# Groups of 768 tokens in an attention and feed-forward kernel: a fourth accumulator, other places for attention work and output stores

## The chip, the cores and the metric

The kernel runs on one core of a Trainium2 chip. The metric is the device time of one execution in microseconds (us): three timed executions of the kernel before took 904.45, 904.82 and 906.39 us, so the median is 904.82. One execution was also taken with a profile.

## The reference

The first part is a windowed attention over 8 batches, 8 heads, 576 positions and head size 64; the second part sends its output, as 4608 tokens of 512 values, through two matrix products with an ELU between them.

```python
scores = scale * np.matmul(q, k.transpose(0, 1, 3, 2))
scores = np.where(masks[None, :, :, :], scores, -1000000000.0)   # window 32, or 128 with stride 4
attn = np.exp(scores - np.max(scores, axis=-1, keepdims=True))
attn = attn / (np.sum(attn, axis=-1, keepdims=True) + 1e-09)
x = np.matmul(attn, v).transpose(0, 2, 1, 3).reshape(4608, 512)
h = x @ w_in                                                      # 512 x 2048
g = np.where(h > 0.0, h, np.exp(np.minimum(h, 0.0)) - 1.0)
return g @ w_out                                                  # 2048 x 512
```

## The kernel before, in words

The 4608 tokens are worked in three chunks of 512 and then in four large groups of 768, each of them two halves of 384 tokens; the program calls the large ones superchunks, and they are numbered c = 0 to 3 here. Nearly all of the time the matrix engine (TensorE, PE in the profile) multiplies, in a fixed order that the program writes down; VectorE (DVE) and ScalarE (ACT) prepare operands, apply the ELU and do the softmax, and SyncE's queue (SP) issues every DMA. Instructions of PE, and those that go through `vec` and `act`, keep the program's order on their engine. Stores, loads and a few others are placed by the scheduler.

A superchunk has 8 steps q. In each step the first product is formed from seven block products, s = 0 to 6, in the order A11, S2, S3, A12, S1, A22, S4 (`ORDER`). Each is six matmuls of 128x384 on a weight block that is streamed from DRAM (`r<-combined`) through a ring of five slots. A11, S2, S3 and A22 add up in one PSUM tile (`x_ps`, h0). A12, S1 and S4 all use the other tile (`y_ps`, h1): A12 and S1 each start it anew and S4 adds to S1. The four results are made by ACT copies u1, u2, u3 of `x_ps` after s = 0, 1, 2; DVE sums C11 = A12 tile + u1 and C22 = S1 tile + u3; an ACT copy C21 of `x_ps` after s = 5; and the DVE sum C12 = S4's tile + u2. The ELU of one step follows in pieces that `TODO` sets beside the products of this step and the next: exponentials and relus (ACT), `elu` (DVE), `cast` (ACT) and `rest` (DVE), which splits a value in a rounded part and a remainder for the next product.

Between the block products PE takes items of the second product from a queue (`pop(n)`: n items of three matmuls of 128x512). `POPS` says how many after each s. Only half of a step's ELU output is used at once. The other half is stored to DRAM (`keep`, `aside`) and comes back in a loop over 16 blocks f at the end of the superchunk (`bring`), in which PE does only second-product items.

Attention for the later batches is woven in. `PIECES` places a scores piece (S, two head pairs: 24 small matmuls, two pops, 48 more) and an output piece (O, 24 small matmuls on `pt`) by 7q + s. After S, DVE adds masks, subtracts the row maximum; ACT takes the exponential; DVE sums, normalises and transposes; ACT copies six blocks to the tile `pt`, which O reads. `work` hands these steps out after each block product, within the time in `SPARE`; `next_step` lets a DVE step run after an ACT step of the same head pair only one place later. Score results use the PSUM tiles a_ps0, a_ps1 and a third one. Between the two halves of S an ACT copy of one column to the tile `nothing` (L523) reads a score.

A finished output tile (128x512) is copied by ACT from PSUM (L645) into one of a few tiles that are used in turn (`out_tiles`), and SP stores it (L646).

Before the first superchunk the last chunk's blocks f = 12 to 15 share DVE and ACT with the making of the seven moving operands (B11, T2, ...; `SOON`, `NEXT`, `FIRST`) and with the first S piece (`EARLY`). `flush` sets how many blocks' second products are left waiting; 16 items are carried into the superchunk.

## Time and profile before

| | us |
|---|---|
| median of three timed runs | 904.82 |
| the profiled execution's own time | 904.12 |
| its span (first to last instruction) | 902.2 |
| PE busy | 868.0 (96% of the span) |
| DVE busy | 586.2 (65%) |
| ACT busy | 529.5 (59%) |
| POOL busy | 6.0 (1%) |

The rows further down come from this execution. A start is in us from the span's start; where an instruction sat idle before, the bracket gives the idle time of its engine and what ended it. Matmuls overlap, so the time one takes from PE is the distance from its start to the next start. TensorE's granted clock is 0.99 to 1.00 of its 2.4 GHz level in every stretch but the one from 326 to 372 us, where the mean is 0.96.

### The profile page before, as it was taken

The numbers are of one execution on the slowest core, as the hardware profiler recorded it, in microseconds if no ns is written. First come the engines' busy times: TensorE is split into PE (matmuls) and PEld (weight loads), VectorE is DVE, ScalarE is ACT, GpSimd is POOL, SyncE is SP. The second block draws the span as 40 slices with busy tenths as digits, with TensorE's granted clock in tenths as the row PEclk, the third lists the DMA queues.
The fourth block names the chain that finished last, engine by engine and source line by source line (L and its number), as shares of the span: only waits on it lengthen the run. The fifth ranks groups of instructions, "written<-read, shape, count | busy, mean of one in ns | idle before, by whom it ended". The sixth has DMA issues, their size and how long they took to land.

```text
span 902.2 us, 17335 instructions
## 1 busy us (share of the span) xinstructions
PE 868.0 (96%) x6752; PEld 714.3 (79%) x6752; DVE 586.2 (65%) x951; ACT 529.5 (59%) x1041; POOL 6.0 (1%) x12
## 2 busy tenths in 40 slices
PE   5999999999999988899999999999999999999998
PEld 4545677778868877788878798888898888999976
DVE  6999998777696976567854657455567446334431
ACT  3665676646555566577774586754476754555541
POOL 2000000000000000000000000000000000000000
PEclk9999999999999999999999999999999999999999
DMA  9996344124546266677753777752676552776541
GB/s 340 381 357 240 120 126 152 60 85 138 179 147 215 74 195 171 212 231 225 234 176 85 237 223 247 206 178 80 216 236 201 163 183 86 211 213 196 160 140 62
DMA packets 93457, 166.46 MB, mean 184 GB/s; under 512 B 9696, under 2 KB 40768, under 8 KB 93376
## 3 DMA queue, kind: packets, MB, share of 16 engines
q1 hardware_dynamic: 93376, 165.36, 57.4%
q8 instruction: 54, 0.88, 0.4%
q14 instruction: 27, 0.22, 0.1%
HBM read 124.42 MB, written 40.89 MB: 183 GB/s over the span
## 4 chain that ended last, share of the span: by engine, by line
PE 63%; DVE 18%; ACT 13%; issue 3%; DMA 3%; SPq 0%; DVEq 0%; ACTq 0%
PE o_ps L112 32%; PE h L112 27%; ACT a L432 6%; PE a_ps L112 3%; DVE a-1_3238 L432 3%; ACT pt L432 2%; DVE pt L419 2%; DMA r<-combined 1%; DVE a L432 1%; DVE a L157 1%; DVE a L155 1%; DVE sums L432 1%; DMA out<-h 1%; DVE r L432 1%; ACT a-1_3238 L432 1%
## 5 line engine op out<-in xcount | busy, mean ns | idle before, releaser
L112 PE MATMUL h<-xall,r 128*128 128x384 f32 (+1 forms) x708 | 154.3, 365 | 4.9 <-DVE a-1_3238 L432 2.3
L112 PE MATMUL o_ps<-a,gh 128*128 128x512 f32 x434 | 147.4, 433 | 0.7 <-ACT gh L614 0.7
L112 PEld LDWEIGHTS h<-xall,r 128*128 128x128 f32 x708 | 127.0, 188 | 23.3 <-DVE a-1_3238 L432 4.7
L112 PE MATMUL h<-r,r 128*128 128x384 f32 x526 | 127.1, 341 | 5.7 <-ACT e L432 2.2
L432 DVE TENSOR_TENSOR a-1_3238<-h,e 128x384 f32<-128x384 f32 x96 | 53.0, 552 | 112.8 <-PE h L112 112.2
L432 ACT ACTIVATE a<-a-1_3238 128x384 f32<-128x384 f32 (+1 forms) x96 | 60.7, 632 | 83.5 <-DVE a-1_3238 L432 82.5
L112 PEld LDWEIGHTS o_ps<-a,gh 128*128 128x128 f32 x434 | 80.6, 188 | 31.5 <-issue 17.2
L112 PEld LDWEIGHTS h<-r,r 128*128 128x128 f32 x526 | 95.0, 189 | 13.0 <-DVE a-1_3238 L432 3.2
L112 PE MATMUL h<-a,r 128*128 128x384 f32 x384 | 93.5, 338 | 0.5 <-ACT e L432 0.5
L432 DVE SCALAR_TENSOR_TENSOR a-1_3238<-a-1_3238,a 128x768 f32<-128x768 f32 x64 | 61.2, 956 | 49.2 <-ACT a L432 49.2
L112 PE MATMUL o_ps<-r,gh 128*128 128x512 f32 x242 | 75.6, 393 | 0.7 <-ACT e L645 0.6
L112 PEld LDWEIGHTS h<-a,r 128*128 128x128 f32 x384 | 68.9, 188 | 7.1 <-ACT e L432 3.6
L432 ACT COPY e<-h 128x384 f32<-128x384 f32 x96 | 45.7, 476 | 49.1 <-PE h L112 46.0
L112 PE MATMUL o_ps<-a,r 128*128 128x512 f32 x288 | 72.4, 392 | 0.0
L112 PE MATMUL o_ps<-a,gl 128*128 128x512 f32 x173 | 67.8, 392 | 0.7 <-DVE gl L615 0.7
L112 PEld LDWEIGHTS o_ps<-a,r 128*128 128x128 f32 x288 | 53.5, 188 | 10.1
L432 ACT ACTIVATE a<-a 128x768 f32<-128x768 f32 (+1 forms) x72 | 60.2, 845 | 1.9
L112 PEld LDWEIGHTS o_ps<-r,gh 128*128 128x128 f32 x242 | 44.7, 188 | 10.1 <-ACT e L645 1.0
L112 PE MATMUL o_ps<-r,gl 128*128 128x512 f32 x117 | 46.0, 393 | 0.7 <-DVE gl L432 0.7
L419 DVE STREAM_TRANSPOSE pt<-sm 32x384 f32<-32x384 f32 x72 | 40.9, 568 | 0.9
L112 PE MATMUL o_ps<-a,xall 128*128 128x512 f32 x153 | 39.7, 394 | 0.0
L601 ACT ACTIVATE e<-h 128x512 f32<-128x512 f32 x44 | 27.1, 618 | 20.0 <-PE h L112 19.4
(191 smaller groups left out, 1356.5 us busy)
## 6 DMA issues: line engine op xcount, KB each, us to landing
r<-combined SPq DMA_DIRECT2D x224, 256.0 KB, 3.2
aside<-a-1_3238 SPq DMA_DIRECT2D x64, 192.0 KB, 2.9
vt<-v SPq DMA_DIRECT2D x30, 384.0 KB, 4.3
kt<-k SPq DMA_DIRECT2D x30, 304.0 KB, 4.6
qt<-q SPq DMA_DIRECT2D x30, 288.0 KB, 4.2
r<-w_in SPq DMA_DIRECT2D x16, 512.0 KB, 7.6
r<-w_out SPq DMA_DIRECT2D x16, 512.0 KB, 7.7
combined<-a SPq DMA_DIRECT2D x20, 256.0 KB, 2.9
```

The costliest lines, as they stand in the source:

```text
L112: return inorder(nc.tensor.matmul(*args, **kw))
L155: keep(nc.vector.scalar_tensor_tensor(out=au, in0=hi, scalar=0xC0000000, in1=au, op0=ALU.bitwise_and, op1=ALU.bitwise_or))
L157: return keep(nc.vector.scalar_tensor_tensor(out=au, in0=lo, scalar=29, in1=au, op0=ALU.logical_shift_right, op1=ALU.bitwise_or))
L419: last_transpose[b] = nc.vector.transpose(out=tr[ks, :, cs], in_=sm[cs, :, rs]).ins
L432: return lambda *args, **kw: inorder(getattr(self.eng, name)(*args, **kw))
L601: a.activation(out=e, in_=h_ps, func=AF.Exp)
```

## The change

- A12 (s = 3) gets an accumulator of its own, a_ps0; S1 and S4 keep h1.
- `POPS` moves two items from behind s = 3 to behind s = 5; the very first step takes four items instead of eight, and 12 items instead of 16 are carried into the first superchunk.
- O pieces move from s = 3 to s = 6 of their step.
- The ACT copy to `nothing` becomes a GpSimd memset of a column of the key tile; the order of the score matmuls and the placing of their results change with it.
- A DVE step after an ACT step comes two places later instead of one (`when + where < turn`), `SPARE` has other numbers, and `keep` comes later in the next step.
- Output stores are issued from ACT's queue once `out_tiles` exists, that is from the first superchunk on.
- The last operands (`NEXT`) are made inside the first step instead of before it; the first S piece comes ahead of the flush, with a flush between its halves.

```diff
-POPS = (2, 2, 0, 2, 0, 0, 0)
-FIRST_POPS = (2, 2, 0, 2, 1, 1, 0)
-TODO = [t.split() for t in ("u1 exp0< relu0< w0", "u2 elu0< keep0< cast1< cast0< rest1< rest0< w1", "u3 w2", "C11 w3", "C22 expR1 w4", "C21 expL1 relu1 w5 push1", "C12 elu1 keep1 w6 push0")]
+POPS = (2, 2, 0, 0, 0, 2, 0)
+FIRST_POPS = (2, 2, 0, 0, 0, 0, 0)
+TODO = [t.split() for t in ("u1 exp0< relu0< w0", "u2 elu0< cast1< cast0< rest1< rest0< w1", "u3 keep1< w2", "C11 w3", "C22 keep0< expR1 w4", "C21 expL1 relu1 w5 push1", "C12 elu1 w6 push0")]
-NEXT = "cast:B21 rest:B21 make:T4 cast:T1 rest:T1".split()
-FIRST = [t.split() for t in ("cast:T4 rest:T4", "cast:B22 rest:B22", "", "", "", "", "")]
+FIRST = [t.split() for t in ("cast:B21 rest:B21", "make:T4 cast:T1 rest:T1", "cast:T4 rest:T4", "cast:B22 rest:B22", "", "", "")]
-PIECES = {0: {14: "S1", 17: "O0", 28: "S2", 31: "O1", 42: "S3", 45: "O2"}, 1: {7: "S4", 28: "S5", 31: "O4", 45: "O5"}, 2: {7: "S6", 28: "S7", 31: "O6", 45: "O7"}}
+PIECES = {0: {14: "S1", 20: "O0", 28: "S2", 34: "O1", 42: "S3", 48: "O2"}, 1: {7: "S4", 28: "S5", 34: "O4", 48: "O5"}, 2: {7: "S6", 28: "S7", 34: "O6", 48: "O7"}}
...
-            ready = (block, pair) not in seen and (where == on_act or when < turn[0]) and not (copies and block - 1 in made)
+            ready = (block, pair) not in seen and (where == on_act or when + where < turn[0]) and not (copies and block - 1 in made)
...
-                nc.scalar.copy(out=nothing, in_=place(1, 0, NU - 1, NU)[:QB, 2 * G - 1:])
+                nc.gpsimd.memset(qk[1][1][:, :1], 0.0)
                 between()
...
-            nc.sync.dma_start(out=out[row:row + P, s], in_=o[:, s])
+            (nc.scalar if out_tiles else nc.sync).dma_start(out=out[row:row + P, s], in_=o[:, s])
...
                 if s == 3:
+                    y_ps = ps_a.tile([P, TC], F32, name="a_ps0")[:, :TH]
+                if s == 4:
                     y_ps = ps_h.tile([P, TC], F32, name="h1")[:, :TH]
...
-        for s in range(3):
+        for s in range(5):
             for what in TODO[s]:
                 if what[-1] == "<":
                     activation(what)
-            pop(2)
+            pop(2 if s < 3 else 0)
...
-            flush(LAG - 1 - (f == NF - 1) if c == 0 and f >= NF - 2 else LAG if c < CS - 1 or f < NF - 2 else LAG + f - (NF - 3))
+            if (c, f) == (CS - 1, EARLY):
+                made[0] = scores_piece(CS + 1, (0, 1), lambda: flush(LAG))
+            flush(LAG - 1 - (f == NF - 1) if c == 0 and f >= NF - 2 else LAG if c < CS - 1 or f < NF - 1 else LAG + 1)
...
-            if (c, f) == (CS - 1, EARLY):
-                made[0] = scores_piece(CS + 1, (0, 1))
...
-            if (c, f) == (CS - 1, NF - 2):
-                for what in NEXT:
-                    moving_operand(0, what, vec, act)
```

PE in superchunk 0, step 4, the first of the two steps there that have both pieces and a full queue; this is the order before, from A12 to S4. h_4169 is the tile of A12, S1 and S4, h_4018 that of the other products, `a_ps<-pt,vt` and `o_ps<-pt,vt` are the O piece.

```order
L112 MATMUL h_4169<-a_1660,r_1073 128x384 [waits DMAHW5_49,DVE_49]
L112 MATMUL a_ps_4180<-pt_80,vt 64x96 [waits DVE_49,PE_49]
L112 MATMUL o_ps_4182<-pt_79,vt 64x96 [waits PE_49]
L112 MATMUL o_ps_3719<-a_1660,gh 128x512 x2
L112 MATMUL o_ps_3806<-a_1660,gh 128x512 x2
L112 MATMUL h_4169<-r_871,r_1073 128x384 [waits DMAHW6_49,DVE_49]
L112 MATMUL h_4018<-xall,r_1073 128x384 [waits DMAHW7_49,Activation_49]
L112 MATMUL h_4169<-xall,r_1073 128x384 [waits DMAHW5_49,DVE_49]
```

And the same place now; a_ps_4171 is the new tile of A12, h_4183 that of S1 and S4.

```order
L110 MATMUL a_ps_4171<-a_1659,r_1072 128x384 [waits DMAHW5_49,DVE_49,PE_49]
L110 MATMUL h_4183<-r_870,r_1072 128x384 [waits DMAHW6_49]
L110 MATMUL h_4020<-xall,r_1072 128x384 [waits DMAHW7_49,Activation_49]
L110 MATMUL o_ps_3719<-a_1659,gh 128x512 x2
L110 MATMUL o_ps_3805<-a_1659,gh 128x512 x2
L110 MATMUL h_4183<-xall,r_1072 128x384 [waits DMAHW5_49,DVE_49]
L110 MATMUL a_ps_4220<-pt_79,vt 64x96 x10
L110 MATMUL o_ps_4222<-pt_78,vt 64x96 [waits PE_49]
```

S1 has no wait on DVE any more, two items stand between A22 and S4, and the O piece has gone from ahead of S1 to behind S4, whose wait on DVE is the one for C22.

ACT in superchunk 1, step 1, before: from the second and third store copy to the copy C21 (`a-1_3238<-h_5065`) and the next step's u1. `sm<-sm` is an attention exponential of the first head pair.

```order
L645 COPY h<-o_ps_4816 128x512 [waits PE_49]
L645 COPY gh<-o_ps_4826 128x512 [waits PE_49]
L432 ACTIVATE sm<-sm 96x768 [waits DVE_49]
L432 ACTIVATE a_2132<-a-1_3238 128x384 [waits DVE_49]
L432 COPY a-1_3238<-h_5065 128x384 [waits PE_49,Activation_49]
L432 COPY e<-h_5266 128x384 [waits PE_49]
```

And now:

```order
L430 ACTIVATE sm<-sm 96x768 [waits DVE_49]
L642 COPY h<-o_ps_4823 128x512 [waits PE_49]
L642 COPY gh<-o_ps_4833 128x512 [waits PE_49]
L643 DMA out<-h 128x512 [waits DMAHW1_49,Activation_49]
L643 DMA out<-gh 128x512 [waits DMAHW2_49,Activation_49]
L430 ACTIVATE a_2131<-a-1_3237 128x384 [waits DVE_49]
L430 ACTIVATE a_2131<-a_2131 96x768
L430 COPY a-1_3237<-h_5072 128x384
```

Two DMA issues, each with a wait for a DMA semaphore, and the second head pair's exponential (96x768) now stand ahead of C21 on ACT.

DVE in superchunk 0, step 0, before: from the last operand remainders (into `xall`) to C22 (`a-1_3238<-h_3495`, the second of the two).

```order
L432 TENSOR_TENSOR xall<-a-1_3238,xall 128x768 [waits PE_49,Activation_49]
L432 TENSOR_TENSOR xall<-x_2832,xall 128x768 [waits PE_49,Activation_49]
L432 TENSOR_REDUCE sums<-sm 96x12
L432 TENSOR_TENSOR a-1_3238<-h_3495,e 128x384 [waits PE_49]
L432 TENSOR_TENSOR sm<-sm,sums 96x768 [waits DVE_49]
L432 TENSOR_TENSOR a-1_3238<-h_3495,e 128x384 [waits PE_49,Activation_49]
```

And now, from the remainder of T1 on, which used to be made before the step:

```order
L430 TENSOR_TENSOR r_870<-a-1_3237,r_870 128x768 [waits Activation_49]
L430 TENSOR_REDUCE nmx<-a_2131 96x12
L430 TENSOR_TENSOR a_2131<-a_2131,nmx 96x768 [waits DVE_49]
L430 TENSOR_TENSOR xall<-a-1_3237,xall 128x768 [waits PE_49,Activation_49]
L430 TENSOR_TENSOR a-1_3237<-a_ps_3503,e 128x384 [waits PE_49]
L430 TENSOR_REDUCE sums<-sm 96x12
L430 TENSOR_TENSOR xall<-x_2831,xall 128x768 [waits Activation_49]
L430 TENSOR_TENSOR a-1_3237<-h_3516,e 128x384 [waits DVE_49,PE_49]
```

The second head pair's maximum and subtraction have moved ahead of the last two operands, and C11 reads a_ps.

## Rows read from the trace of the kernel before

**Rows 1.** The profile page: the chain of work that ended last, by engine, as shares of the span.

```profile
PE 63%; DVE 18%; ACT 13%; issue 3%; DMA 3%; SPq 0%; DVEq 0%; ACTq 0%
```

**Rows 2.** Busy time by stretch: the stretch and its length; then for PE, PEld, DVE, ACT and POOL the busy us and number of instructions; PE clock, DMA share, GB/s. The rows are the whole program in seven parts, and then three stretches for themselves: superchunk 0, step 4 up to the end of S4, and a step without attention work.

```profile
0.00:326.00 326.00, 310.42 (x2728) 226.99 (x2731) 273.72 (x430) 191.46 (x408) 6.03 (x12) 0.99 0.55 188
326.00:372.00 46.00, 37.05 (x400) 31.47 (x384) 27.43 (x46) 29.46 (x55) 0.00 (x0) 0.96 0.56 167
372.00:461.00 89.00, 88.07 (x816) 76.11 (x813) 65.47 (x113) 63.80 (x123) 0.00 (x0) 1.00 0.71 222
...
399.00:412.05 13.05, 12.81 (x186) 11.04 (x169) 9.57 (x17) 8.08 (x19) 0.00 (x0) 1.00 0.80 262
804.28:815.74 11.46, 11.46 (x61) 10.67 (x61) 4.62 (x8) 6.25 (x12) 0.00 (x0) 1.00 0.65 194
```

**Rows 3.** Who PE waited for from 326 us to the end: total us, times, longest.

```profile
PE h L112 <- ACT e L432: 2.7, 3, 2.2
PE h L112 <- ACT nothing L523: 1.0, 1, 1.0
```

**Rows 4.** Instructions in order of time on PE from 328 us to the second step of superchunk 0 (start, us, what, idle before).

```profile
328.14 3.01 PE L112 MATMUL h<-xall,r 128*128 128x512 f32 x12
337.19 0.44 PE L112 MATMUL h<-r,r 128*128 128x384 f32 x1 [2.23 <-ACT e L432]
355.32 1.55 PE L112 MATMUL o_ps<-r,r 128*128 128x512 f32 x6
356.71 1.21 PE L112 MATMUL h<-r,r 128*128 128x384 f32 x6
357.75 1.21 PE L112 MATMUL h<-xall,r 128*128 128x384 f32 x6
361.30 1.32 PE L112 MATMUL h<-xall,r 128*128 128x384 f32 x6 [2.34 <-DVE a-1_3238 L432]
363.68 2.29 PE L112 MATMUL h<-r,r 128*128 128x384 f32 x6 [1.06 <-ACT a-1_3238 L432]
383.48 1.20 PE L112 MATMUL h<-r,r 128*128 128x384 f32 x6
```

**Rows 5.** DVE and ACT in the same stretch: operand work, the ELU of the last block, and a store copy that waits for its tile.

```profile
334.55 0.95 DVE L432 TENSOR_TENSOR r<-a-1_3238,r 128x768 fp32r<-128x768 f32 x1
335.42 0.68 DVE L432 SCALAR_TENSOR_TENSOR e<-h,e 128x512 f32<-128x512 f32 x1
358.38 0.95 DVE L432 TENSOR_REDUCE sums<-a 96x12 f32<-96x768 f32 x1 [2.30 <-ACT a L432]
362.25 0.59 ACT L645 COPY h<-o_ps 128x512 f32<-128x512 f32 x1 [3.44 <-DMA out<-h]
```

**Rows 6.** Superchunk 0, steps 3 and 4: the ends of step 3 and the copies to `pt` (ACT), the chain on DVE from the masks to C22, and O on PE.

```profile
395.51 0.56 DVE L432 TENSOR_TENSOR a-1_3238<-h,e 128x384 f32<-128x384 f32 x1 [0.95 <-PE h L112]
396.48 0.96 DVE L432 SCALAR_TENSOR_TENSOR a-1_3238<-a-1_3238,a 128x768 f32<-128x768 f32 x1 [0.41 <-ACT a L432]
399.11 3.10 ACT L432 COPY pt<-a 32x384 f32<-32x384 f32 x6
402.24 0.75 DVE L432 TENSOR_TENSOR a<-o_ps,masks_sb 96x256 f32<-96x256 f32 x2 [4.80 <-ACT pt L432]
410.41 0.55 DVE L432 TENSOR_TENSOR a-1_3238<-h,e 128x384 f32<-128x384 f32 x1
405.08 1.87 PE L112 MATMUL a_ps<-pt,vt 128*64 128x96 f32 x40
407.21 0.73 PE L112 MATMUL o_ps<-a,gh 128*128 128x512 f32 x2
```

**Rows 7.** Superchunk 1, step 4, for the same places: C12 of the step before and the masks on DVE, and the first product of step 5 on PE.

```profile
539.88 0.56 DVE L432 TENSOR_TENSOR a-1_3238<-h,e 128x384 f32<-128x384 f32 x1 [1.47 <-PE h L112]
544.75 0.75 DVE L432 TENSOR_TENSOR a<-o_ps,masks_sb 96x256 f32<-96x256 f32 x2 [2.95 <-PE o_ps L112]
555.69 0.51 PE L112 MATMUL h<-r,r 128*128 128x384 f32 x2
```

**Rows 8.** Superchunk 1, step 6, which has an O piece and no scores: the start of O on PE and the start of the items behind it.

```profile
574.59 1.21 PE L112 MATMUL a_ps<-pt,vt 128*64 128x96 f32 x24
577.34 1.66 PE L112 MATMUL o_ps<-a,r 128*128 128x512 f32 x6
```

**Rows 9.** The start of the loop over f in superchunk 1.

```profile
598.84 1.42 PE L112 MATMUL o_ps<-r 128*128 128x512 f32 x5 [0.33 <-DVE r L432]
```

**Rows 10.** Superchunk 1, step 1 (scores, no O): PE and SP; the last two rows are DMA issues that start at 508.78 and at 509.26, with KB and us to landing.

```profile
514.84 1.30 PE L112 MATMUL h<-xall,r 128*128 128x384 f32 x6 [0.74 <-DVE sums L432]
516.64 1.30 PE L112 MATMUL h<-r,r 128*128 128x384 f32 x6 [0.50 <-DMA r<-combined]
511.91 0.91 SPq L646 DMA_DIRECT2D out<-h  x1
r<-combined SPq DMA_DIRECT2D x1, 256.0 KB, 5.9
out<-h SPq DMA_DIRECT2D x1, 256.0 KB, 6.1
```

**Rows 11.** The last instructions of the program: ACT's store copies and SP's issues.

```profile
897.19 1.27 ACT L645 COPY h<-o_ps 128x512 f32<-128x512 f32 x2 [8.55 <-PE o_ps L112]
898.95 0.86 SPq L646 DMA_DIRECT2D out<-gh  x2
```

More of the change, by code (lines that the diff above doesn't have):

```diff
@@ L51 @@
 MOVING = "B11 T2 T3 B21 T1 T4 B22".split()
-POPS = (2, 2, 0, 2, 0, 0, 0)
-FIRST_POPS = (2, 2, 0, 2, 1, 1, 0)
-TODO = [t.split() for t in ("u1 exp0< relu0< w0", "u2 elu0< keep0< cast1< cast0< rest1< rest0< w1", "u3 w2", "C11 w3", "C22 expR1 w4", "C21 expL1 relu1 w5 push1", "C12 elu1 keep1 w6 push0")]
-SPARE = ((1.4, 0.4), (0.3, 0.9), (1.2, 1.7), (1.8, 1.7), (0.7, 0.0), (0.8, 0.0), (0.0, 0.0))
+POPS = (2, 2, 0, 0, 0, 2, 0)
+FIRST_POPS = (2, 2, 0, 0, 0, 0, 0)
+TODO = [t.split() for t in ("u1 exp0< relu0< w0", "u2 elu0< cast1< cast0< rest1< rest0< w1", "u3 keep1< w2", "C11 w3", "C22 keep0< expR1 w4", "C21 expL1 relu1 w5 push1", "C12 elu1 w6 push0")]
+SPARE = ((1.4, 0.45), (0.3, 0.9), (1.2, 1.3), (1.6, 1.7), (0.9, 0.5), (0.9, 0.0), (0.0, 0.45))
 SOON = "cast:B11 make:T1 rest:B11 make:T2 cast:T2 rest:T2 make:T3 cast:T3 rest:T3".split()
-NEXT = "cast:B21 rest:B21 make:T4 cast:T1 rest:T1".split()
-FIRST = [t.split() for t in ("cast:T4 rest:T4", "cast:B22 rest:B22", "", "", "", "", "")]
+FIRST = [t.split() for t in ("cast:B21 rest:B21", "make:T4 cast:T1 rest:T1", "cast:T4 rest:T4", "cast:B22 rest:B22", "", "", "")]
 OPERANDS = [t.split() for t in ("", "", "", "cast:B11", "make:T1 rest:B11", "make:T2 cast:T2", "rest:T2 make:T3", "cast:T3 rest:T3", "cast:B21 rest:B21", "make:T4 cast:T1",
@@ L91, in body @@
     ident = const.tile([QB, QB], F32, name="ident")
-    nothing = const.tile([QB, 1], F32, name="nothing")
     pt = [const.tile([P, 2 * NU, QB], F32, name=f"pt{i}") for i in range(2)]
@@ L501, in steps @@
                     ks, cs, rs = slice((c + r) * G, (c + r + 1) * G), slice(c * G, (c + 1) * G), slice(r * G, (r + 1) * G)
-                    yield True, True, 0.45, lambda ks=ks, cs=cs, rs=rs: act.copy(out=tr[ks, :, cs], in_=sm[cs, :, rs])
+                    yield True, True, 0.51, lambda ks=ks, cs=cs, rs=rs: act.copy(out=tr[ks, :, cs], in_=sm[cs, :, rs])
         block = BLOCKS.index((b, hps[0]))
@@ L512, in place @@
         def place(j, h, n0, n1):
-            bank, o = (s[h], n0 + j * NU) if j == 0 or n0 < 2 else (s[2], n0 - 2 + h * 4)
+            bank, o = (s[2], n0 + h * 4) if j and n0 < 4 else (s[h], n0 + 2 * j)
             return bank[:, o * 2 * G:(o + n1 - n0) * 2 * G]
@@ L519, in scores_piece @@
         one, other = [(0, n) for n in range(NU)], [(1, n) for n in range(NU)]
-        for i, (first_head, second_head) in enumerate(zip(other[2:] + other[:2] + one, other[:2] + one + other[2:])):
+        for i, (first_head, second_head) in enumerate(zip(other[1:4] + other[:1] + other[4:] + one, other[4:] + one + other[:4])):
             if i == 4:
-                nc.scalar.copy(out=nothing, in_=place(1, 0, NU - 1, NU)[:QB, 2 * G - 1:])
+                nc.gpsimd.memset(qk[1][1][:, :1], 0.0)
                 between()
-            for c in range(GU):
+            for c in range(GU)[::-1 if i == 3 else 1]:
                 for h, (j, n) in enumerate((first_head, second_head)):
                     score(place(j, h, n, n + 1), *qk[j], h, n, c)
-        groups = [[[(n0, n1, place(j, h, n0, n1)) for n0, n1 in (((0, NU),), ((2, NU), (0, 2)))[j]] for h in range(2)] for j in range(2)]
+        groups = [[[(n0, n1, place(j, h, n0, n1)) for n0, n1 in (((0, NU),), ((0, 4), (4, NU)))[j]] for h in range(2)] for j in range(2)]
         if b <= CS:
```

## Prediction

> **What bounds the kernel now.** I read the page's chain first. PE alone carries 63% of the span, and DVE and ACT another 31% [rows 1], so PE is the bound and the others matter where they make it wait. The split into stretches says where that is [rows 2]: from 326 to 372 us PE is idle for 46.00 - 37.05 = 8.95 us, from 372 to 461 us for 0.93, and a step without attention work has none: 11.46 us, 11.46 busy. The accumulator for A12 can therefore give nothing in plain steps. What can move is the transition into the first superchunk, the steps with attention pieces, the superchunks' ends and the tail. The waits [rows 3] and the rows in order of time give each its size.
>
> The unit prices, by distance of starts: a block product 357.75 - 356.71 = 1.04 us, two items of the second product 356.71 - 355.32 = 1.39 [rows 4], an O piece 407.21 - 405.08 = 2.13 [rows 6].
>
> **The transition.** The flush inside S puts one block's four items (2.8 us) where PE waited 1.0 for `nothing` [rows 3]; the last block's product then ends at about 332.7 rather than 331.0. Operand work no longer stands ahead of its ELU on DVE, as it did until 335.42 [rows 5]; that ELU needs 1.9 us of ACT behind the product, so it starts at 334.6 and u1, two casts later, is done at 336.4, when PE has done a product and four items and wants it. The 2.23 of idle at 337.19 goes [rows 4]. But five operand instructions of about 0.9 (335.42 - 334.55, [rows 5]) now lie on DVE inside the step, with the softmax's maximum, subtraction and sum between. Adding them up from 336.6, T1 is ready at 341.4, T4 at 344.2, B22 at 346.6 and C22 at 347.1. PE wants them at 341.1, 342.5 and 345.2, and so waits 0.3, 1.7 and 1.9, and S4 ends at 348.2, where it ended near 348.5. Nearly all is given back.
>
> In the next step the sum over the second head pair no longer sits ahead of C22 waiting 2.30 for its exponential (358.38, [rows 5]); the 2.34 and 1.06 behind it [rows 4] go. Against that u3 stands behind two store copies (0.59 each) and two issues (0.4 each), a wait of 0.5, so the step ends at about 360.3 instead of near 362.4. In step 2 the second pair's copies to `pt` end at 368.5, and masks, DVE chain, S4 and O (worked out below) end it at 380.4; the next step's first product stood at 383.48. Sum: **-3.0**. Bounds: -8.9 if the whole idle time goes, +2 if the second pair of store copies, which waits for the first pair's landing as at 362.25 (3.44, [rows 5]), holds C21 and u1 again.
>
> **O behind S4.** Before, 2.13 us of O stood ahead of S1 and gave C11 and C22 time. Now only two items (1.39) stand between A22 and S4. In superchunk 0, step 4, the masks start when ACT has copied `pt` out of the tile they write (402.24), and from there to the end of C22 DVE needs 410.96 - 402.24 = 8.7 us [rows 6], in an order that the change keeps. Measured from the end of S4 of the step before (395.5): exponential and relu no longer wait for the 0.41 ahead of `elu`, nor for `nothing`, so the masks start at 6.3 instead of 6.7; C22 is ready at 15.0, S4 ends at 16.1, O at 18.2. Before, S4 ended at 412.05, which is 16.55: +1.65. PE would have had its work done at 12.8, so 2.2 us of it is plain waiting. Steps 4 and 6: +3.3. In superchunks 1 and 2, step 4, no copies are in the way and the masks start behind the scores, 544.75 - 539.85 = 4.9 after S4: C22 at 13.6, O's end at 16.8, against 555.69 - 539.85 = 15.8 [rows 7], +1.0 each. Step 2 is in the transition. Sum: **+5.3**, bounds +0.5 (the masks at 4.9 everywhere and C22 sooner) and +8.5 (four times 2.13).
>
> **Steps with O alone** (superchunks 1 and 2, step 6): O took 577.34 - 574.59 = 2.75 us [rows 8], 0.6 more than elsewhere, because it caught up with the copies to `pt`; at the end of the step they have 6 us more: twice 0.6, **-1.2**, bounds -1.2 and 0.
>
> **Ends of superchunks.** The first items of the loop wait for a cast and then 0.33 for `rest` on DVE [rows 9]. The chain that leads there (C12, `elu`, exponential, relu, `elu`, cast, `rest`) gains the 0.41 before `elu` [rows 6], since two items now part C21 from S4 and relu is done by then, and a little of ACT. Of some 0.7 per end 0.5 goes, four times: **-2.0**, bounds -2.8 and 0.
>
> **Small waits** for u1 and u2 behind ACT's attention work (2.7 less the 2.23 of the transition, [rows 3]): **-0.5**, bounds -1 and +1.
>
> **Stores from ACT.** The trace has no DMA issue on ACT; the nearest rows are SP's, 0.43 (half of 0.86, [rows 11]) to 0.91 [rows 10]. Between 0.4 and 0.9 for some 26 stores lies beside idle time of ACT (59% busy) except where a u or C copy follows at once. Superchunk 1, step 1, is such a place (and its twin in superchunk 2). There the two later issues stand ahead of expR, of an exponential and of C21. Each waits for a DMA semaphore: one for a weight block (issued 508.78, 5.9 to land, so 514.7), the other for the step's first store, which took 6.1 [rows 10]. If that holds, ACT goes on at 515.5, C21 ends at 517.3 and the next step starts 0.7 later than its 516.64. If the waits are over in time, C21 is early, the weights issued behind the stores on SP come 0.4 to 0.9 sooner, and the 0.74 [rows 10] shrinks: -0.7. S4's weights land at 514.7 either way. Between +0.8 and -0.7 per step I take **0**; bounds for both, -1.4 and +1.6.
>
> The Trainium skill, page "DMA: Bandwidth & Descriptors", section "Issuing engines are not separate DMA queues", says that DMAs issued by ScalarE or SyncE run on the same 16 engines and that spreading them saves only the sequencer's time for issuing. By that rule the weight blocks land no sooner for bytes' sake, and these steps would stand at 0 or above; by the 0.91 that an issue took on SP they could gain up to 0.7 each. The rule speaks against this part of the change, and no run here shows yet which holds.
>
> **Tail.** Copies and issues now alternate on one engine: copy 897.2 to 897.8, issue 0.4, copy 0.59, half copy 0.37, three issues, so the last issue ends near 900.4 instead of 899.8 [rows 11]: **+0.6**, bounds 0 and +1.2.
>
> **`nothing` and the memset.** 0.15 of ACT goes, twelve times, its two long waits are counted in the transition, and POOL is idle (6 us busy in all, [rows 2]): 0 here, and nothing is queued behind the memset. `keep` later on SP: 0, since its data are needed only at the superchunk's end.
>
> **Sum:** -3.0 + 5.3 - 1.2 - 2.0 - 0.5 + 0 + 0.6 = -0.8 us. Against the profiled execution, 904.12 (span 902.2), that is 903.3; the median of the runs stands 0.7 above that execution, so **904.0**. What a measurement can tell from no change is about 0.2%, 1.8 us: 903.0 to 906.6.
>
> **Rivals.**
> - *The masks come early.* If the copies to `pt` are over by the end of the scores in superchunk 0 as well, its two O steps end at 16.8 as in the later ones and cost 0.25 instead of 1.65, and the transition, whose step 2 hangs on the same copies and whose DVE order is tight, gives 6 rather than 3: -0.8 - 2.8 - 3 = -6.6, **898.2**. For it: the second exponential is issued within its own step now, so all that follows can come earlier. Against: in the order, the six copies still stand behind the next step's relu.
> - *ACT stalls on its own issues* (slower than before). One mechanism: a store that waits for its DMA semaphore holds every copy and exponential behind it on ACT. Two steps at +0.8 instead of 0, and the transition's gain lost, as its second pair of stores waits for the first: -0.8 + 1.6 + 3.0 = +3.8, **908.6**. It decides from about 1.5 us between a store's copy and its issue. For it: landings of 6 us in these steps, and the order shows the waits. Against: before the stores of most steps DMAs are sparse, and the semaphore they wait for is old.
> - *Hidden anyway.* All that goes is cover for something that is late next, the weights or the DVE chain, and the O steps find work too: **904.8**.
>
> **How the numbers follow.** The forecast's own case, gains and O's price nearly cancelling (900.5 to 906.5), has 0.48: faster 0.18, no change 0.25, slower 0.05. Masks early 0.25, faster. ACT stalls 0.19, slower. Hidden 0.08: 0.02, 0.04, 0.02. Together faster 0.45, within 0.2% 0.29, slower 0.26. The range leaves out the far ends of both rivals: 896 to 909.5; the forecast's own is 900.5 to 906.5.
>
> **What would show it.** In the new profile: no wait for `nothing`; between 335 and 350 us PE waiting for operand remainders on DVE (`xall`, `r`); in superchunk 0, steps 4 and 6, about 2 us of idle time of PE ahead of S4, released by DVE; the first waits of each f loop at 0.2 instead of 0.7; ACT's issues taking 0.4 with gaps up to 3 us ahead of them in step 1 of superchunks 1 and 2. I am wrong if S4 doesn't wait in these O steps, if step 0 of superchunk 0 has no operand waits, or if plain steps differ from 11.46.

## The result and the profile after

The kernel after takes 910.22 us (median; 908.71 to 916.70), the kernel before 904.49 on the same chips (903.79 to 906.39). The ratio is 1.0067, with a 95% interval of 1.0048 to 1.0086: 5.7 us slower. The prediction came to 904.0, and its range ended at 909.5.

The profiled execution of after took 912.36 us, 2.1 more than its median, with a span of 910.6. The page, with the busy times, ACT's new DMA queue (q10: packets, MB, share of 16 engines) and the chain by engine:

```profile
PE 871.8 (96%) x6752; PEld 719.5 (79%) x6752; DVE 584.0 (64%) x951; ACT 529.4 (58%) x1029; POOL 7.2 (1%) x24
...
q10 hardware_dynamic: 4176, 7.34, 2.2%
...
PE 70%; DVE 13%; ACT 9%; issue 4%; DMA 3%; SPq 1%; ACTq 0%; POOL 0%; DVEq 0%
```

PE is still the bound. Its busy time rose by 3.8 us, from 868.0, though it does the same work: either its matmuls ran slower somewhere or they count waits. Who PE waited for from 326 us to the end (compare [rows 3]):

```profile
PE h L110 <- DVE a-1_3237 L430: 7.7, 5, 2.1
PE h L110 <- DMA r<-combined: 4.3, 2, 2.5
PE h L110 <- ACT a-1_3237 L430: 2.4, 2, 1.2
PE h L110 <- issue: 1.6, 1, 1.6
PE h L110 <- DVE xall L430: 1.4, 1, 1.4
```

The waits for `nothing` and nearly all of those for `e` are gone. In their place stand five waits for DVE (the steps with S and O), two for a weight block and two for C21 from ACT; the last four lie in step 1 of superchunks 1 and 2. The busy time by stretch shows what followed there (columns as in [rows 2]):

```profile
326.00:372.00 46.00, 42.84 (x464) 36.54 (x463) 29.55 (x53) 30.98 (x55) 0.20 (x2) 0.93 0.63 186
...
512.00:519.00 7.00, 4.52 (x25) 3.94 (x24) 5.98 (x8) 2.57 (x5) 0.00 (x0) 1.00 0.98 340
519.00:522.00 3.00, 1.80 (x9) 1.49 (x8) 0.56 (x1) 2.48 (x5) 0.00 (x0) 0.85 1.03 363
522.00:526.00 4.00, 4.00 (x16) 3.58 (x15) 3.20 (x6) 2.57 (x4) 0.00 (x0) 0.69 0.48 159
526.00:530.00 4.00, 4.00 (x23) 3.74 (x22) 2.95 (x6) 2.39 (x6) 0.00 (x0) 1.00 0.50 145
804.00:815.46 11.46, 11.46 (x62) 10.67 (x61) 4.52 (x7) 6.19 (x11) 0.00 (x0) 1.00 0.72 216
```

From 512 to 519 us PE is busy for 4.52 of 7.00, then the granted clock goes to 0.85 and 0.69: part of that time the engine ran at 1.2 GHz. The stretch from 522 is fully busy and yet does only 16 matmuls in 4.00, where the next does 23. A plain step is still 11.46 us.

Next, where the difference lies. The lengths are worked out from the starts of each step's first block product in the two traces; "forecast" is the prediction's term.

| part (profiled executions, us) | before | after | difference | forecast |
|---|---|---|---|---|
| start of step 3 of superchunk 0 (all of the transition before it) | 383.5 | 382.4 | -1.1 | -3.0 |
| steps with S and O: superchunk 0 steps 4 and 6; superchunks 1 and 2 step 4 | 16.85, 16.87; 16.01, 16.01 | 19.03, 19.03; 16.79, 16.80 | +5.9 | +5.3 |
| steps with O alone (superchunks 1 and 2, step 6) | 14.46, 14.46 | 13.68, 13.68 | -1.6 | -1.2 |
| steps 7 with the loops behind them | 48.10, 45.09, 45.09, 53.03 | 48.27, 45.13, 45.11, 52.91 | +0.1 | -2.0 |
| superchunk 1, steps 1 and 2; superchunk 2, the same | 16.14, 11.56; 15.60, 11.54 | 17.75, 13.12; 17.04, 12.97 | +6.0 | 0 |
| the other steps, small waits | | | -1.4 | -0.5 |
| last matmul to the span's end | 4.1 | 4.4 | +0.3 | +0.6 |
| span | 902.24 | 910.57 | +8.3 | -0.8 |

The fifth line decides. The end of step 1 of superchunk 1 in order of time: PE (the last items, S4, the next step), then ACT, then the SP issue of S4's weights.

```profile
514.62 1.55 PE L110 MATMUL o_ps<-r 128*128 128x512 f32 x6
518.65 1.29 PE L110 MATMUL h<-xall,r 128*128 128x384 f32 x6 [2.48 <-DMA r<-combined]
521.13 2.29 PE L110 MATMUL h<-r,r 128*128 128x384 f32 x6 [1.20 <-ACT a-1_3237 L430]
523.22 2.15 PE L110 MATMUL o_ps<-a,r 128*128 128x512 f32 x6
```

```profile
515.51 0.59 ACT L642 COPY h<-o_ps 128x512 f32<-128x512 f32 x1
516.20 0.59 ACT L642 COPY gh<-o_ps 128x512 f32<-128x512 f32 x1
518.59 0.34 ACTq L643 DMA_DIRECT2D out<-h  x1
519.02 0.39 ACTq L643 DMA_DIRECT2D out<-gh  x1
519.46 0.53 ACT L430 ACTIVATE a<-a-1_3237 128x384 f32<-128x384 f32 x1 [2.67 <-DMA r<-combined]
...
520.62 0.46 ACT L430 COPY a-1_3237<-h 128x384 f32<-128x384 f32 x1
...
511.88 0.38 SPq L728 DMA_DIRECT2D r<-combined  x1
...
r<-combined SPq DMA_DIRECT2D x1, 256.0 KB, 6.6
```

Read it from below: S4's weights were issued at 511.88 and landed 6.6 later, at 518.5. At 518.59 the first of ACT's two store issues went out, and at 518.65 S4 began. The bracket on the next row names a DMA of weights as what ended ACT's idle time, and it is the same block: in the trace the issue waits for the semaphore that this block's landing raises. The store has nothing to do with the weights; the program uses a few DMA semaphores in turn. ACT had ended its store copy at 516.8, and the 2.67 of the bracket run from there to 519.46. Behind the two issues stand expR (an exponential of the ELU), the second head pair's exponential and C21 (520.62). C21 has to empty the PSUM tile for the next step, so PE stood 1.20 more, and then did step 2 at the lower clock: the six matmuls of 128x512 from 523.22 have 2.15 beside them where the same form takes 1.55.

The step with S and O, superchunk 0 step 4: the masks and C22 on DVE, S4 and O on PE.

```profile
400.86 0.75 DVE L430 TENSOR_TENSOR a<-o_ps,masks_sb 96x256 f32<-96x256 f32 x2 [4.84 <-ACT pt L430]
...
409.02 0.55 DVE L430 TENSOR_TENSOR a-1_3237<-h,e 128x384 f32<-128x384 f32 x1
...
409.62 1.32 PE L110 MATMUL h<-xall,r 128*128 128x384 f32 x6 [2.14 <-DVE a-1_3237 L430]
410.87 1.87 PE L110 MATMUL a_ps<-pt,vt 128*64 128x96 f32 x40
```

The masks begin behind the copies to `pt` as before [rows 6], C22 is done at 409.6, and PE has stood idle 2.14 for it with O (410.87) still to do.

The transition: PE's two waits for operands in the first step, and the stretches at and behind them.

```profile
345.16 1.15 PE L110 MATMUL h<-xall,r 128*128 128x384 f32 x5 [1.40 <-DVE xall L430]
347.87 2.26 PE L110 MATMUL h<-xall,r 128*128 128x384 f32 x6 [1.56 <-issue]
...
347.00:351.00 4.00, 3.13 (x10) 3.16 (x11) 3.44 (x8) 2.25 (x4) 0.00 (x0) 0.50 0.27 70
351.00:355.00 4.00, 4.00 (x15) 3.53 (x14) 2.69 (x4) 2.07 (x3) 0.00 (x0) 0.64 0.70 188
```

The clock fell there too, to 0.50 and 0.64. A fall of this kind comes and goes from execution to execution: step 1 of superchunk 0 takes 13.41 us in this one and 11.51, 12.02 and 12.06 in three profiles below (stores on SP, idle time filled, stores issued late), whose kernels differ from this one up to there in the stores' queue or in nothing. In two of these (idle time filled, stores issued late) the clock stays at 1.00 and step 3 begins at 378.7 and 378.5, nearly 4 us sooner than the 382.4 of the table; both are the fastest of their twelve executions, 3.0 us below their medians, where this one is 2.1 above its own. The kernel before had a fall as well:

```profile
361.00:367.00 6.00, 4.64 (x61) 3.72 (x61) 2.71 (x5) 3.73 (x7) 0.00 (x0) 0.72 0.67 231
```

So a profile by itself settles up to 4 us in the transition badly. Below, the medians decide on totals, and the profiles on the steps behind the transition.

### The profile page after: what moved, and what is told of

Read it like the earlier page. It is cut to its first block, busy times and chain, and to the rows that moved or that the text cites. A ratio compares the mean times of both kernels' runs of the same rounds, so it can differ in the third digit from the quotient of the medians.

```text
span 910.6 us, 17336 instructions
## 1 busy us (share of the span) xinstructions
PE 871.8 (96%) x6752; PEld 719.5 (79%) x6752; DVE 584.0 (64%) x951; ACT 529.4 (58%) x1029; POOL 7.2 (1%) x24
## 4 chain that ended last, share of the span: by engine, by line
PE 70%; DVE 13%; ACT 9%; issue 4%; DMA 3%; SPq 1%; ACTq 0%; POOL 0%; DVEq 0%
PE o_ps L110 34%; PE h L110 29%; PE a_ps L110 6%; ACT a L430 2%; DVE a-1_3237 L430 2%; ACT pt L430 2%; DMA r<-combined 2%; DVE pt L417 1%; DVE sm L430 1%; ACT h L642 1%; DVE nmx L430 1%; DVE sm L312 1%; DVE nmx L394 1%; DVE r L430 1%; DVE sm L381 1%
## 5 line engine op out<-in xcount | busy, mean ns | idle before, releaser
L110 PE MATMUL h<-xall,r 128*128 128x384 f32 (+1 forms) x708 | 160.2, 367 | 16.7 <-DVE a-1_3237 L430 7.7
L110 PE MATMUL h<-r,r 128*128 128x384 f32 x476 | 112.7, 347 | 2.4 <-ACT a-1_3237 L430 2.4
L110 PEld LDWEIGHTS h<-r,r 128*128 128x128 f32 x476 | 86.8, 193 | 6.5 <-ACT a-1_3237 L430 3.0
L430 DVE TENSOR_TENSOR a-1_3237<-h,e 128x384 f32<-128x384 f32 x64 | 35.5, 554 | 71.6 <-PE h L110 71.6
L110 PE MATMUL h<-a,r 128*128 128x384 f32 x256 | 60.5, 337 | 0.5 <-ACT e L430 0.5
L110 PEld LDWEIGHTS h<-a,r 128*128 128x128 f32 x256 | 46.1, 188 | 5.6 <-ACT e L430 1.8
L430 DVE TENSOR_TENSOR a-1_3237<-a_ps,e 128x384 f32<-128x384 f32 x32 | 17.7, 554 | 43.9 <-PE a_ps L110 43.9
```

The source lines that it names most:

```text
L110: return inorder(nc.tensor.matmul(*args, **kw))
L430: return lambda *args, **kw: inorder(getattr(self.eng, name)(*args, **kw))
```

## The experiments

The theory after the first reading: the loss has two parts that add up, the stores on ACT (by their place, and then by the clock) and O behind S4. The rivals: the lower clock is a cause by itself or only the picture of something else; or the queue, not the place, makes the stores dear; or the transition is the loser. Each kernel was timed beside the kernel before, whose medians lay between 904.07 and 904.59; differences from the kernel after are differences of medians from separate sessions.

**Stores back on SP.**

```diff
-            (nc.scalar if out_tiles else nc.sync).dma_start(out=out[row:row + P, s], in_=o[:, s])
+            nc.sync.dma_start(out=out[row:row + P, s], in_=o[:, s])
```

> The changed kernel with the output stores back on SP's queue. Theory 'stores': in step 1 of superchunks 1 and 2 two stores on ACT wait for DMA semaphores and hold C21, the first of them gets ahead of S4's weight block, and the idle time lowers TensorE's clock in step 2. Then steps 1 and 2 of those superchunks (17.75 and 13.12 us, 17.04 and 12.97) go back to at most 16.2 and 11.6, and the kernel is about 5 us faster than the changed one: 904 to 906. Rival 'weights': the weight block of S4 is late because PE comes to it earlier, whoever issues the stores; then steps 1 and 2 stay within 0.5 us of what they are, and the time stays at 909 to 911.

Measured: 903.28 us, ratio to before 0.9986 (0.9975 to 0.9998); 6.9 us under the kernel after. Steps 1 and 2 take 15.54 and 11.87 in superchunk 1, 15.20 and 11.59 in superchunk 2, and steps 7 with their loops 47.78, 44.72 and 44.72. So the stores on ACT cost 6.9 us, more than all of the loss.

**O at s = 5.**

```diff
-PIECES = {0: {14: "S1", 20: "O0", 28: "S2", 34: "O1", 42: "S3", 48: "O2"}, ...
+PIECES = {0: {14: "S1", 19: "O0", 28: "S2", 33: "O1", 42: "S3", 47: "O2"}, ...
```

> The changed kernel with the O piece behind A22 (s = 5), ahead of the two items and of S4, instead of behind S4. Theory 'cover': O behind S4 leaves PE 2.3 us of idle time ahead of S4 in superchunk 0, steps 2, 4 and 6, and 0.8 in step 4 of superchunks 1 and 2; ahead of S4, O fills it up to its own wait for C11, so these steps get shorter by 0.9 to 2.1 and by 0.8 each: 4 to 6 us less in all, 904.5 to 906.5. Rival: O waits for C11 (it writes a_ps0) or its results hold the step's other ACT copies, and the wait only changes its place: steps within 0.4 us, time 909 to 911.

Measured: 903.57 us, ratio 0.9983 (0.9968 to 0.9998). Steps 4 and 6 of superchunk 0 go from 19.03 to 18.08, step 4 of the later ones from 16.79 to 16.03. That is 3.4 us of a difference of 6.7 in the medians. Some of the rest is not this edit's: step 2 of superchunk 2 took 11.60 in this profile without a fall of the clock. Some may be falls that the waits ahead of S4 bring in other executions: with the stores on SP and O still behind S4, step 2 of superchunk 0 took 21.43 (19.06 in after), with a clock of 0.75 and 0.82 behind its wait. How much, no run shows. The stores were still on ACT here, and C21 was late by the same 1.20 in step 1, although S4's weights came 0.9 and 0.2 us sooner: step 1 took 16.82 and 16.81. Between these two kernels the weights' landing and the clock vary, the wait for C21 doesn't.

**Stores on ACT in the kernel before.** The same line as in the first edit, the other way round, in the kernel before and nothing else.

> The kernel before with nothing changed but that the output stores are issued from ACT's queue. Theory 'stores': step 1 of superchunks 1 and 2 gets longer by 1 to 2 us, and step 2 too if the clock falls: 3 to 6 us slower than before, 907.5 to 910.5. Rival 'weights' (it needs the own accumulator to do harm): within 1 us of before, 903.5 to 905.5.

Measured: 906.80 us, ratio 1.0026 (1.0014 to 1.0038): 2.2 us more than the kernel before, less than the theory's 3 to 6 and more than the rival's 1. The place that the theory named is not where it lies. Step 1 takes 15.68 and 15.84, against 16.14 and 15.60 before: no loss. ACT there:

```profile
513.37 0.34 ACTq L646 DMA_DIRECT2D out<-h  x1
513.75 0.58 ACT L645 COPY gh<-o_ps 128x512 f32<-128x512 f32 x1 [1.04 <-DMA kt<-k]
...
515.31 0.34 ACTq L646 DMA_DIRECT2D out<-gh  x1
...
516.57 0.46 ACT L432 COPY a-1_3238<-h 128x384 f32<-128x384 f32 x1
```

The issues wait here as well (1.04 for a DMA), but they stand early in the step, behind the items at s = 3, and C21 is copied when S4 needs it. What the stores do cost is in steps 7 with their loops (48.62, 45.44 and 45.44 against 48.10, 45.09 and 45.09; the last 53.37 against 53.03) and perhaps in step 2 of the transition (20.82 against 19.79, which one profile settles badly). So a store on ACT costs something everywhere in the loops, and much only where its place is ahead of C21.

**The same stores, issued behind C21.** In step 1 of superchunks 1 and 2 the three stores are kept back and issued by ACT after the copy C21.

```diff
-            (nc.scalar if out_tiles else nc.sync).dma_start(out=out[row:row + P, s], in_=o[:, s])
+            if hold[0]:
+                held.append((out[row:row + P, s], o[:, s]))
+            else:
+                (nc.scalar if out_tiles else nc.sync).dma_start(out=out[row:row + P, s], in_=o[:, s])
...
+                hold[0] = c in (1, 2) and q == 1 and s < 6
+                if c in (1, 2) and q == 1 and s == 6:
+                    for to, src in held:
+                        with tc.issue_after(c21):
+                            nc.scalar.dma_start(out=to, in_=src)
...
```

> The changed kernel, all stores still on ACT's queue, but the three of step 1 in superchunks 1 and 2 are issued behind C21 instead of right behind their copies. Theory 'place': it is not the queue that costs but that these issues stand ahead of C21 and that the first store leaves ahead of S4's weight block; then steps 1 and 2 get as short as with the stores on SP (15.5 and 11.9, 15.2 and 11.6 us), and the kernel is 4 to 6 us faster than the changed one: 904 to 906. Rival 'queue': stores on a second queue slow the weight blocks down wherever they are issued; then step 1 stays above 17 and the time at 909 to 911.

Measured: 904.59 us, ratio 0.9997 (0.9986 to 1.0008): 5.6 us of the 6.9 come back from moving six issues, and all stores are still ACT's. Steps 1 and 2 take 15.42 and 11.55, and 15.50 and 11.54; the loops keep their 48.32, 45.11 and 45.10. PE and ACT at the end of step 1:

```profile
513.77 1.28 PE L110 MATMUL h<-xall,r 128*128 128x384 f32 x6 [1.50 <-DMA r<-combined]
514.90 0.94 PE L110 MATMUL h<-r,r 128*128 128x384 f32 x4
```

```profile
513.44 0.83 ACT L430 ACTIVATE a<-a 96x768 f32<-96x768 f32 x1
513.72 0.34 ACTq L811 DMA_DIRECT2D out<-h  x1
514.17 0.46 ACT L430 COPY a-1_3237<-h 128x384 f32<-128x384 f32 x1
```

S4 still waits 1.50 for its weights (2.48 in after), so most of that wait is not the stores'. But expR and the exponential are past, C21 runs beside S4, and the next step follows at once. In the program's order all three issues stand behind C21; that the second begins at 513.72, ahead of C21's 514.17, shows that an issue can begin on ACT's sequencer while a copy ahead of it still waits for its turn.

The edit moves a second thing: the first store, which in after left before S4's weights were issued, now comes behind them. The block took 5.5 and 5.4 us to land here, 6.6 and 6.1 in after; over all thirteen profiles it took 5.9 to 6.6 in the ten of these steps where a store from ACT went out ahead of it or with it, and 5.4 to 6.0 in the sixteen others. No run separates the two, but S4 starts only 1.0 and 0.2 us later in after, where step 1 is 2.3 and 1.5 longer.

**The idle time filled.** Twelve more matmuls whose results nothing reads, ahead of S4 in the same two steps; the stores stay as in the kernel after.

```diff
+                if s == 5 and q == 1 and c in (1, 2):
+                    fill = ps_a.tile([P, TC], F32, name="a_ps1")[:, :TH]
+                    product(base + s, fill, True)
+                    product(base + s, fill, True)
```

> The changed kernel with twelve more matmuls (two products that are written to an unused tile and never read, 2.1 us of PE work) ahead of S4 in step 1 of superchunks 1 and 2, where PE is idle for 2.5 us. It computes the same output. Theory 'clock': the long step 2 (13.1 us against 11.5) comes from the half clock that follows the idle time; filled, the clock stays at 1.00 and step 2 takes 11.6 or less, so in spite of more work the kernel is 2 to 3 us faster than the changed one: 907 to 908.5. Rival: step 2 is long because ACT and the weights are late; then it stays near 13 and the time at 910 or above.

Measured: 906.88 us, ratio 1.0023 (1.0010 to 1.0036): more work, and 3.3 us faster than the kernel after. The twelve matmuls, and the stretches from them on:

```profile
512.33 2.25 PE L110 MATMUL a_ps<-xall,r 128*128 128x384 f32 x12
...
508.20:515.20 7.00, 7.00 (x40) 6.74 (x39) 5.98 (x8) 3.50 (x7) 0.00 (x0) 1.00 0.96 330
...
518.20:522.20 4.00, 4.00 (x22) 3.65 (x21) 3.79 (x8) 2.98 (x5) 0.00 (x0) 1.00 0.72 227
```

PE is busy for 7.00 of 7.00 where it was for 4.52, and the clock stays at 1.00: steps 2 take 11.57 and 11.59 instead of 13.12 and 12.97, 2.9 us less in this profile, where the medians differ by 3.3. The wait for C21 fell too, from 1.20 to 0.43 and 0.35, since ACT's issues were held less long here and S4 starts behind the filling; so both idle times shrank. Step 1 got shorter as well, 16.33 and 16.25; its weights landed sooner in this execution, so that part doesn't count for the clock.

**Items at s = 3 again.** The kernel after with the items' old place and all else as it is.

```diff
-POPS = (2, 2, 0, 0, 0, 2, 0)
+POPS = (2, 2, 0, 2, 0, 0, 0)
```

> The kernel after with one edit: POPS is (2, 2, 0, 2, 0, 0, 0) again, so the two items that stood behind A22 in each step stand behind A12. Question: does the harm of the ACT stores need the items behind s = 5, whose store copies and issues come just ahead of C21? Theory 'place': yes. With the items at s = 3 the step's later stores are issued about 3 us sooner, ahead of C21 by more than a landing, so step 1 of superchunks 1 and 2 goes from 17.75 and 17.04 to about 15.7, and step 2 from 13.1 and 13.0 to about 11.6: -6.5 us against the kernel after in these steps. In steps with O at s = 6 nothing but S4 would stand between A22 and O, so these waits grow by up to 0.7 each, four times: +2.8 at most. Together 904 to 906.5. Rival 'any store on ACT in these steps': steps 1 and 2 keep their length and the time is 909 to 913.

Measured: 914.76 us, ratio 1.0117 (1.0097 to 1.0136), 4.5 slower than after: outside both expectations. Steps 1 take 16.38 and 16.03 and steps 2 take 11.91 and 11.95, so the theory is half right where it looked. But the third store's issue waited there as well:

```profile
519.88 0.34 ACTq L643 DMA_DIRECT2D out<-gh  x1
```

which is 2.2 us after the copy that it stores had ended (517.7). The rest was misjudged: the items between A22 and S4 are needed in more steps than the ones with O. Steps 5 go from 11.59 to 11.96, step 3 of superchunk 0 the same, the loops to 48.97, 45.61 and 45.61, and step 6 of superchunk 0 from 19.03 to 21.01, where the wait for C22 is followed by O at a lower clock (the mean over this step is 0.92):

```profile
440.55 1.32 PE L110 MATMUL h<-xall,r 128*128 128x384 f32 x6 [2.29 <-DVE a-1_3237 L430]
441.80 3.36 PE L110 MATMUL a_ps<-pt,vt 128*64 128x96 f32 x40
```

The plain steps of superchunk 3 stay at 11.46. The items' new place is thus a gain of the change in the other steps and loops.

**Both costs taken out.** Stores on SP and O at s = 5 together.

> The changed kernel with both: stores on SP's queue and O pieces behind A22 (s = 5). Theory: the two costs lie in different steps and add up: 903.3 and 903.6 against 910.2 make 896 to 898.5. Rival: they share the clock's falls, and what is left is little more than one of them: 901 to 903.5.

Measured: 897.28 us, ratio 0.9925 (0.9911 to 0.9939). The two costs add up: 910.22 less 6.9 and less 6.7 would be 896.6.

**Old order where S and O share a step.** Stores on SP; in the five steps with both pieces A12 shares h1, the items are at s = 3 and O is at s = 3, as before; all other steps as after.

```diff
...
+                    shared = 7 * q + 3 in PIECES.get(c, {})
+                    y_ps = (ps_h.tile([P, TC], F32, name="h1") if shared else ps_a.tile([P, TC], F32, name="a_ps0"))[:, :TH]
...
-                pop((FIRST_POPS if (c, q) == (0, 0) else POPS)[s] - (2 if what[:1] == "S" else 0))
+                pop((FIRST_POPS if (c, q) == (0, 0) else (2, 2, 0, 2, 0, 0, 0) if 7 * q + 3 in PIECES.get(c, {}) else POPS)[s] - (2 if what[:1] == "S" else 0))
```

> The changed kernel with stores on SP's queue, and in the five steps that have scores and O both, the order of the kernel before (A12 in the tile of S1 and S4, two items and O behind A12), the own accumulator elsewhere. Theory: steps 4 and 6 of superchunk 0 go back from 19.0 to 16.9 and step 4 of the later two from 16.8 to 16.0; with step 2 it is 6 to 8 us less than with the stores alone moved: 895.5 to 898. Rival: the steps are bound by the DVE chain in any order, within 1 us of 903.

Measured: 896.82 us, ratio 0.9914 (0.9896 to 0.9932): faster than both kernels of this study. Steps 4 and 6 of superchunk 0 take 16.93 and 16.96 (19.03 in after), step 4 of the later ones 16.47 and 16.46, where the theory had 16.0.

**The new transition in the kernel before.** `NEXT`, `FIRST`, `FIRST_POPS` and the flush with S inside it, nothing else of the change.

> The kernel before with only the new way into the first superchunk: T1, B21 and T4 made inside its first step, the first S piece ahead of the flush with a flush between its halves, four items instead of eight in the first step, 12 carried instead of 16. By my sum of the transition: 0 to 2.5 us faster than before, 902 to 904.5. Rival: the operand work inside the step costs more than the stall it removes, 905 to 907.

Measured: 904.75 us, ratio 1.0006 (0.9995 to 1.0017): neither a gain nor a loss.

**The old transition in mixed_steps.** The reverse edit.

> The kernel of mixed_steps with the transition of the kernel before: the last operands are made ahead of the first step, 16 items are carried in, the first scores piece stands behind the flush. Question: is the transition's term (-3.0 in the prediction, nothing where it was put into the kernel before by itself) there when the rest of the change is in? Theory 'none': the time stays at 896.8 within 1. Rival 'with A12 apart': the new transition needs A12's own accumulator and the stores' new places, and gives 2 to 4 here: 899 to 901.

Measured: 895.40 us (893.75 to 898.63), ratio 0.9906 (0.9887 to 0.9926), against 0.9914 (0.9896 to 0.9932) with the new one: no difference that can be told. A gain of 3.0 would have shown in either company.

**One place instead of two in mixed_steps.**

```diff
-            ready = (block, pair) not in seen and (where == on_act or when + where < turn[0]) ...
+            ready = (block, pair) not in seen and (where == on_act or when < turn[0]) ...
```

> The kernel of mixed_steps with the old rule for the attention steps: a DVE step after an ACT step of the same head pair may come one place later instead of two. Question: what does the rule of two places give? Theory 'cover': two places keep DVE from standing idle for an exponential in front of C22 or C12 (2.30 us in the transition, 0.4 to 0.5 elsewhere); with one place the six steps with scores get 0.3 to 0.5 us longer each and the transition up to 2.3: 898.5 to 901. Rival 'hidden': the SPARE budgets put the step two places later anyway, and the time stays at 896.8 within 1.

Measured: 897.77 us, ratio 0.9934 (0.9918 to 0.9950). The interval overlaps with that of mixed_steps, and step by step the two profiles differ by 0.3 at most outside the transition (16.95 and 16.96 in step 6 of superchunk 0). If the rule gives anything it is under 2 us; neither expectation can be told from the other at that size.

## Why the prediction was wrong, point by point

**The step that failed is "Stores from ACT", taken as 0 with bounds of -1.4 to +1.6.** Its mechanism was in the text: two issues ahead of expR, of an exponential and of C21, one of them held until a weight block lands. What it measured is +6.0 in steps 1 and 2 of superchunks 1 and 2, and 6.9 us in the medians with and without it. Three things make up the difference.
- The weights. The text had them land 14.2 us behind the step's start (514.7 less 500.5) and ACT going on 0.8 after that. In the profile of after they landed at 15.1 in superchunk 1 (518.5 less 503.4) and at 14.4 in superchunk 2; S4 began at 13.8 to 14.3 in the profiles of late stores, SP stores and O at s = 5. So 0.9 of the growth of one step and 0.2 of the other is a landing that varies. Why it was so late in this execution wasn't settled, though a store from ACT ahead of the block went with a longer landing, as said above.
- The hold. Its price was near: with O at s = 5, where the weights landed at 14.2, step 1 took 16.82 and 16.81, 0.7 and 1.2 more than before, for the +0.8 of the text. It is the 1.20 that PE waits for C21 in both steps, there and in after, and not at all with the stores behind C21; in the kernel before, PE waited 0.50 at this place for weights [rows 10]. This price was worked out and then averaged away.
- The clock. The idle time of the two waits together brought 1.2 GHz into step 2, 1.6 and 1.4 us in this profile, half of the +6.0. No term had it, though the kernel before showed 0.96 in the stretch with the most idle time [rows 2]. It doesn't follow each time: with O at s = 5 the same two waits did so in superchunk 1 and not in superchunk 2.

The wrong choice was the value in the middle: "if that holds" was the very row that the order showed, and the other end rested on SP's 0.91. The rule of the Trainium skill, page "DMA: Bandwidth & Descriptors", section "Issuing engines are not separate DMA queues", that spreading issues over engines saves only the time for issuing, stood against this part of the change, and the trace agrees as far as it goes: S4's weights landed no sooner with the stores on ACT (6.6 after the issue here, 5.9 in [rows 10]). But most of the cost wasn't in the transfers: the same stores from the same queue, a little later in ACT's order, cost 5.6 us less.

**Ends of superchunks, -2.0: gained, and given back.** With the stores on SP steps 7 with their loops shrink by 0.3 to 0.5 each (47.78 for 48.10, 44.72 for 45.09 twice, 52.52 for 53.03), -1.6 in sum; with the stores on ACT it is +0.1. Where it goes can be seen on PE and ACT in the loop of superchunk 1:

```profile
608.48 0.39 PE L110 MATMUL o_ps<-r,gl 128*128 128x512 f32 x1
608.92 0.74 PE L110 MATMUL o_ps<-r,gh 128*128 128x512 f32 x2
```

```profile
607.49 0.34 ACTq L643 DMA_DIRECT2D out<-h  x1
607.87 0.51 ACT L430 CAST gh<-r 128x384 fp32r<-128x384 f32 x1 [0.41 <-ACT h L642]
608.29 0.58 ACT L642 COPY h<-o_ps 128x512 f32<-128x512 f32 x1
```

The cast stands behind a store's issue, and the next store copy, which frees a PSUM tile that PE is to write, behind the cast. That copy ends at 608.87, and the item starts 0.44 after the last instead of 0.23; in the trace its weight load waits for ACT's semaphore. "Between 0.4 and 0.9 for some 26 stores lies beside idle time of ACT" was therefore wrong in the loops. The first wait did shrink, from 0.33 [rows 9] to 0.16, as the prediction said it would.

**O behind S4, +5.3: right.** +5.9 in the profile, from the mechanism given: masks at 6.9 us behind the end of the step before (forecast 6.3), S4 ends at 16.9 (16.1), O at 19.0 (18.2), 2.1 of plain waiting ahead of S4. With O in its old place and order these steps got shorter by 2.1 us in superchunk 0 and by 0.3 in the later ones, with O at s = 5 by 0.95 and 0.8.

**The transition, -3.0: not there in the medians.** Its working held in part: the waits in the first step came (1.40 and 1.56 for 1.7 and 1.9; the profile puts the second down to `issue`, but C22 on DVE ended at 347.8, just ahead of it), step 2 waited 2.13 ahead of S4, and the whole is -1.1 in this profile. The sum had no term for the clock, which fell to 0.50 and 0.64 of full speed over 8 us behind these waits. In the two executions without a fall the whole is -4.8 and -5.0, against a kernel before that had a fall itself. Alone and taken away the new transition measures 0 in the medians; where the gain goes in the other executions isn't shown.

**O alone (-1.2), small waits (-0.5), tail (+0.6), `nothing`, plain steps:** -1.6, -1.4, +0.3, no wait for `nothing` left, 11.46. Right, or a little better than forecast. The small waits gained more since the items between A22 and S4 give ACT and DVE time in the steps beside attention work, which the items at s = 3 showed (steps 5 longer by 0.37, of which PE waits 0.21 for C21 at the end).

**The rivals.** "ACT stalls on its own issues", 908.6, happened in its first half: by its place, and by the point it named (more than 1.5 us between a store's copy and its issue; here 516.1 to 518.59, 2.5). Its second half, the transition's gain lost to the stores (+3.0), didn't: with the stores on SP step 3 of superchunk 0 began at 382.9, no sooner. And it missed the clock and the loops. That it ends 1.6 us short in all is luck. "The masks come early" didn't happen: they start when the copies to `pt` end, as before.

## What to carry to other kernels

On ScalarE a DMA issue was an instruction with a wait, and what stood behind it in the engine's order waited too (2.67 us in step 1): before moving issues there, read what stands behind each and how old the semaphore is that it waits for, and put the issue behind the next result that the bound engine needs. Where an added wait lies beside another one on the matrix engine, price the clock as well as the wait: twice 1.5 us came from there in this case. And when several edits come together, a small net change can hide gains and losses of 7 us each; undoing them one at a time gave a kernel 0.9% faster than before.

## What was unexpected of the hardware

TensorE's granted clock fell behind a stretch in which the engine stood idle for 2.5 us of 7 and then for 1.2 of 3, to a mean of 0.69 over the 4 busy us that followed, and filling the gap with useless matmuls made the program 3.3 us faster. But a wait of 2.1 to 2.3 ahead of S4 in superchunk 0 left it at 1.00 in the kernel after and not with the items at s = 3, and in the same place it fell in one superchunk and not in the other (step 2 took 13.16 in superchunk 1 and 11.60 in superchunk 2 with O at s = 5). What decides between these isn't settled by the runs.
